# A block mask spread by GpSimd, mask rows in fewer head pairs, and token mixing moved ahead

## The chip, the cores and the metric

The kernel runs on one core of a Trainium2 chip. The metric is the device time of one execution in microseconds (us). A profile is one execution, and its span is about 2 us shorter than the device time.

The engines are PE (TensorE, matmuls), PEld (TensorE's weight loads), ACT (ScalarE), DVE (VectorE), POOL (GpSimd) and SP (SyncE).

## The reference, cut to what matters

Block-sparse attention (4 batches, 8 heads, 768 positions, head size 64) is followed by an MLP mixer over tokens and channels.

```python
scores = scale * np.matmul(q, k.transpose(0, 1, 3, 2))
blk_i, blk_j = pos[:, None] // 32, pos[None, :] // 32
mask = np.abs(blk_i - blk_j) <= 1
mask = mask | (blk_i == 0) | (blk_j == 0) | (blk_i == n_blocks - 1) | (blk_j == n_blocks - 1)
for qb in range(n_blocks):                       # three sampled key blocks per query block
    for kb in sampled_blocks[qb]:
        mask[qb*32:(qb+1)*32, kb*32:(kb+1)*32] = True
attn = softmax(np.where(mask, scores, -1e9))
x = (attn @ v)                                   # then to (batch, position, 512)
h = np.maximum(xt @ w_tok1, 0.0) @ w_tok2        # xt: x transposed, mixing of positions
u = x + h.transpose(0, 2, 1)
out = u + np.maximum(u @ w_ch1, 0.0) @ w_ch2     # mixing of channels
```

The mask is made of blocks: all positions of one query block have the same mask column.

## The kernel before: the parts that matter

The 32 heads are worked in 16 pairs. One pair has 9 attention steps, one exponential each, 144 in all. I number the steps from 1 and the pairs from 0. A batch is four pairs.

The mask is applied in two ways. In the first `NT0 = 6` pairs the scores matmul has 24 more contraction rows, which add a large negative number where a key block is not allowed. From pair 6 on, the scores have only 64 rows. Two heads' matmuls then share the array, two steps are issued together, and VectorE multiplies the exponentials by a 0/1 tile, `mask`.

```python
ev = P.op(("act",), {"act": 948.0}, [done], exp, prio=0, lat=80.0)
if p >= NT0:
    def cut(eng):                                # the mask product
        nc.vector.tensor_tensor(out=ets[s]..., in0=ets[s]..., in1=free(mask[...]), op=ALU.mult)
    ev = P.op(("dve",), {"dve": 740.0}, [ev, mask_there], cut, prio=5)
```

That tile comes from 12 matmuls of 384 columns, each with an eviction by VectorE:

```python
def mask_stream():
    for j in range(NC):                          # 6
        for hf in range(2):
            ...
                nc.tensor.matmul(out=box["m"][:, 0:384], lhsT=ind[R, j, :],
                                 rhs=qtb[0][R, 0, 384 * hf : 384 * hf + 384], ...)
            ...
                nc.vector.tensor_scalar(out=mask[:, j, 384 * hf : 384 * hf + 384],
                                        in0=box["m"][:, 0:384], scalar1=-1.0, ..., op0=ALU.is_ge)
```

The order of instructions on each engine is fixed when the kernel is built. A planner steps through estimated time. TensorE takes work from the stream with the lowest number that is ready: scores 0, PV 1, transposes 2, token mixing 3, channel mixing 4, mask 1.8. Loads go into one list, which GpSimd issues in order:

```python
for p in range(4, NP):
    loads.append(p)                              # k, q, v of pair p, when their buffers are free
    if p == 5:
        loads.append(load_ch1)                   # weights of the first channel matmul
    if p == 7:
        loads.append(load_ch2)                   # weights of the second
```

In the traces each engine then does its list in order, and if one instruction waits, what stands behind it on that engine waits too: the 1.23 us wait of one VectorE copy, shown below, holds up the two adds behind it.

The softmax here doesn't subtract the row's maximum and nothing guards it: scores larger than these inputs give would overflow.

Of the kernel before, what the change touches and what calls it, by code (L numbers as in the profile page):

```python
# [50 lines left out]
class Planner:  # L51
# [52 lines left out]
    def step(self):  # L104
# [3 lines left out]
        if self.free_at["pe"] <= self.now:  # L108
            for s in self.streams:
# [11 lines left out]
                if t <= self.now:  # L121
                    s[3] = None
                    emit()
                    if self.trace is not None:
                        self.trace.append((self.now, "pe", s[0], cost))
                    self.free_at["pe"] = self.now + cost
                    if done is not None:
                        done.t = self.now + cost + self.PE_LAT + self.SEM
                    moved = True
                    break  # L130
# [43 lines left out]
def kernel(  # L174
# [12 lines left out]
    nc = tc.nc  # L187
# [11 lines left out]
    NT0 = 6  # L199
# [226 lines left out]
    rows_there = {p: Ev(START) for p in range(NV)}  # L426
    ones_there = [Ev(START) for _ in range(NV)]

    def first_rest():
# [33 lines left out]
        rows_there[0] = e2_there  # L463
        for n in range(1, NV):
# [10 lines left out]

    mask = sb1.tile([128, NC, S], BF16, name="mask")
    mask_there = Ev()

    def mask_stream():

        for j in range(NC):
            for hf in range(2):
                box, last, rel = {}, Ev(), Ev()

                def emit(j=j, hf=hf, box=box, rel=rel):
                    P.take("pm", rel)
                    box["m"] = psM.tile([128, 512], FP32, tag="pm", name=f"pm_mask_{j}_{hf}")
                    nc.tensor.matmul(  # L488
                        out=box["m"][:, 0:384], lhsT=ind[R, j, :],
                        rhs=qtb[0][R, 0, 384 * hf : 384 * hf + 384], start=True, stop=True,  # L490
                    )

                yield 162.5, [Ev(34 * US), rows_there[0]], [("pm", 1)], emit, last

                def copy(eng, j=j, hf=hf, box=box):
                    nc.vector.tensor_scalar(
                        out=mask[:, j, 384 * hf : 384 * hf + 384], in0=box["m"][:, 0:384],
                        scalar1=-1.0, scalar2=None, op0=ALU.is_ge,
                    )

                ev = P.op(("dve",), {"dve": 556.0}, [last], copy, prio=4)
                rel.same_as = ev
        mask_there.same_as = ev
# [124 lines left out]
    def scores(s, done, rel):  # L628
# [24 lines left out]
        if p >= NT0:  # L653
            def cut(eng):
                nc.vector.tensor_tensor(  # L655
                    out=ets[s][:, :, :].rearrange("k h (i q) -> k h i q", i=2),
                    in0=ets[s][:, :, :].rearrange("k h (i q) -> k h i q", i=2),
                    in1=free(mask[:, 2 * jj, 256 * t : 256 * t + 256], 0, [[0, 2], [S, 2], [1, 256]]),
                    op=ALU.mult,
                )  # L660

            ev = P.op(("dve",), {"dve": 740.0}, [ev, mask_there], cut, prio=5)
# [40 lines left out]
    def pv_stream():  # L703
        for s in steps:
# [3 lines left out]
            def emit(s=s, done=done):  # L708
# [39 lines left out]
                ev = P.op(("dve",), {"dve": 630.0}, [done], norm, prio=1)  # L748
# [42 lines left out]
    def tok(b, g):  # L791
        deps = [x_there[2 * g + 4 * b + i, h] for i in range(2) for h in range(3)] + [tok1_there]
        box = {}
# [19 lines left out]
        a_there = relu_op(lambda: a_t[:, :, :], box["pm"][:, :, :], [last], 3)  # L813
        alias(rel, a_there)
        u_evs = []
        for s2 in range(3):
# [22 lines left out]
            ev = P.op(("dve",), {"dve": 695.0}, [last], add, prio=3)  # L839
# [6 lines left out]
        for dmc in (2 * g, 2 * g + 1):  # L846
# [25 lines left out]
            ev = P.op(("dve", "act"), {"dve": 555.0, "act": 740.0}, [last], evac, prio=3)  # L872
# [86 lines left out]
    def tok_stream():  # L959
        for b in range(B):  # L960
# [10 lines left out]
    P.stream(3, tok_stream())  # L971
# [5 lines left out]
    for p in range(4, NP):  # L977
# [3 lines left out]
        if p == 7:  # L981
            loads.append(load_ch2)

    def pull():
        while loads:
            x = loads[0]
            if callable(x):
                x(P.now)
# [42 lines left out]
```

## Time and profile before

| | before |
|---|---|
| device time, median of 3 runs | 263.84 us (263.08 to 264.56) |
| span of the profile | 261.9 us |
| busy share PE / DVE / ACT / POOL | 97% / 66% / 69% / 16% |
| mask matmuls and their evictions | 12 of 384 columns, 12 x 549 ns on VectorE |
| mask products on VectorE | 90 x 682 ns |
| granted TensorE clock, mean | 1.000 |

The chain of work that ended last shows what the end time hangs on. The timeline of ScalarE shows when each attention step ran and what it waited for. The waits say which instruction stood, and on what.

### The profile page before, as it was taken

What the parts mean: (1) busy time and instruction counts of PE and PEld (TensorE: products, weight loads), DVE (VectorE), ACT (ScalarE), POOL (GpSimd) and SP (SyncE); (2) the same over time, 40 slices, a digit from 0 to 9 for tenths busy, and PEclk for the clock granted to TensorE, in tenths of its full rate; (3) what the DMA queues carried; (4) which work ended last, traced back from release to release, by engine and by line L of the source; (5) the groups of instructions that cost most, each with busy time, mean ns of one, the idle gap of its engine ahead of it and who ended that gap; (6) DMA issues with size and microseconds to landing.
All of it is one profiled execution on the core that took longest, in us unless ns stands there. A gap on an engine that the chain in (4) does not pass through costs nothing.

```text
span 261.9 us, 6584 instructions
## 1 busy us (share of the span) xinstructions
PE 253.7 (97%) x2769; PEld 166.3 (63%) x2787; DVE 172.2 (66%) x386; ACT 179.4 (69%) x227; POOL 42.0 (16%) x66
## 2 busy tenths in 40 slices
PE   8898999999999999999999999999999999999994
PEld 3587987897766666567556765566565554565444
DVE  7887788787988889788888888888841012200222
ACT  5899999999887887677777887777407730177100
POOL 8845555462303010000000000000000000000000
PEclk9999999999999999999999999999999999999999
DMA  6999999999665726141735030015214003200122
GB/s 145 191 216 202 213 201 206 204 200 190 92 100 78 98 33 120 44 103 40 167 99 40 3 60 3 0 43 103 78 46 100 0 8 115 94 28 3 40 107 95
DMA packets 39262, 25.58 MB, mean 98 GB/s; under 512 B 20480, under 2 KB 35600, under 8 KB 39232
## 3 DMA queue, kind: packets, MB, share of 16 engines
q0 software_dynamic: 15104, 12.98, 31.7%
q1 hardware_dynamic: 23856, 11.97, 19.4%
q8 instruction: 22, 0.36, 0.6%
q10 hardware_dynamic: 272, 0.20, 0.3%
q14 instruction: 8, 0.07, 0.1%
HBM read 26.74 MB, written 6.29 MB: 126 GB/s over the span
## 4 chain that ended last, share of the span: by engine, by line
PE 85%; DMA 6%; DVE 4%; POOL 2%; issue 1%; POOLq 0%
PE pm_ch L893 24%; PE pm_ch L919 23%; PE ps L637 15%; PE po L723 13%; DMA vraw<-in_v_dram 6%; PE pm_tok L801 4%; PE pm_tok L826 4%; PE pm_mask L488 1%; DVE x L834 1%; DVE et L655 1%; PE tk L579 1%; PE tq L579 1%; PE pm_ut L855 0%; DVE x L738 0%; DVE ktb L608 0%
## 5 line engine op out<-in xcount | busy, mean ns | idle before, releaser
L647 ACT ACTIVATE et<-ps 128x1024 bf16<-128x1024 f32 x144 | 139.1, 1024 | 28.0 <-PE ps L637 26.7
L893 PE MATMUL pm_ch<-uT,w_ch 128*128 128x384 bf16 x384 | 70.1, 326 | 0.0
L919 PE MATMUL pm_ch<-w_ch,rc 128*128 128x512 bf16 (+2 forms) x294 | 67.0, 362 | 1.1 <-issue 0.3
L637 PE MATMUL ps<-qtb,ktb 64*128 64x256 bf16 (+1 forms) x576 | 60.4, 272 | 1.1 <-ACT et L647 0.7
L723 PEld LDWEIGHTS <-et 128*128 128x128 bf16 x1152 | 49.3, 97 | 17.0 <-issue 3.1
L655 DVE TENSOR_TENSOR et<-et,mask 128x1024 bf16<-128x1024 bf16 x90 | 57.8, 682 | 0.0
L723 PE MATMUL po<-vaug,et 128*128 128x65 bf16 x1152 | 56.1, 193 | 1.2 <-DVE x L738 0.8
L765 ACT ACTIVATE rc<-pm_ch 128x384 bf16<-128x384 f32 x69 | 33.8, 492 | 26.9 <-PE pm_ch L893 26.7
L931 DVE TENSOR_TENSOR o<-pm_ch,x 128x512 f32<-128x512 f32 x23 | 15.8, 687 | 52.6 <-PE pm_ch L919 52.6
L893 PEld LDWEIGHTS <-w_ch 128*128 128x128 bf16 x384 | 35.4, 98 | 22.0 <-issue 2.2
L637 PEld LDWEIGHTS <-ktb 64*128 64x128 bf16 (+1 forms) x576 | 32.6, 95 | 18.5 <-issue 13.5
L919 PEld LDWEIGHTS <-rc 128*128 128x128 bf16 x312 | 27.5, 98 | 24.8 <-issue 1.3
L738 DVE TENSOR_TENSOR x<-po,recip 128x256 bf16<-128x256 f32 x48 | 20.4, 424 | 1.7
L737 DVE RECIPROCAL recip<-po 128x4 f32<-128x4 f32 x48 | 8.7, 181 | 19.3 <-PE po L723 18.8
L834 DVE TENSOR_TENSOR x<-pm_tok,x 128x512 bf16<-128x512 f32 x24 | 15.7, 682 | 4.1 <-PE pm_tok L826 4.1
L234 POOL DMA_DIRECT2D vraw<-in_v_dram x16 | 11.6, 727 | 32.7 <-DVE vaug L525 27.8
L767 DVE TENSOR_SCALAR rc<-pm_ch 128x384 bf16<-128x384 f32 x27 | 14.8, 552 | 2.2 <-PE pm_ch L893 1.8
L826 PE MATMUL pm_tok<-a_t,w_tok 128*128 128x256 bf16 x96 | 14.1, 276 | 0.2
L801 PE MATMUL pm_tok<-x,w_tok 128*128 128x256 bf16 x96 | 13.6, 273 | 0.0
L234 POOL DMA_DIRECT2D qraw<-in_q_dram x15 | 10.8, 721 | 8.0 <-DMA w_tok<-in_moe_w_tok_dram 1.9
L234 POOL DMA_DIRECT2D kraw<-in_k_dram x15 | 10.8, 719 | 7.0 <-DVE klay L528 1.8
L826 PEld LDWEIGHTS <-w_tok 128*128 128x128 bf16 x96 | 9.9, 128 | 1.5 <-issue 1.0
(71 smaller groups left out, 116.1 us busy)
## 6 DMA issues: line engine op xcount, KB each, us to landing
out_dram<-o SPq DMA_DIRECT2D x23, 256.0 KB, 2.1
vraw<-in_v_dram POOLq DMA_DIRECT2D x16, 192.0 KB, 7.1
w_ch<-in_moe_w_ch_dram POOLq DMA_DIRECT2D x8, 384.0 KB, 9.9
kraw<-in_k_dram POOLq DMA_DIRECT2D x15, 192.0 KB, 8.3
qraw<-in_q_dram POOLq DMA_DIRECT2D x15, 192.0 KB, 7.3
w_tok<-in_moe_w_tok_dram POOLq DMA_DIRECT2D x2, 384.0 KB, 9.8
kf<-in_k_dram SPq DMA_DIRECT2D x2, 192.0 KB, 3.0
ktb<-ktb SPq DMA_DIRECT2D x3, 72.0 KB
```

The source lines that it names most:

```text
L234: nc.gpsimd.dma_start(out=raw[:, :, :, :], in_=APx(src, 2 * p * S * D, [[NC * D, 128], [S * D, 2], [1, NC * D]]),)
L637: nc.tensor.matmul(out=ps[:, hd, 256 * i : 256 * i + 256], lhsT=ktb[n][rows, h, 256 * jj + 128 * i : 256 * jj + 128 * i + 128], rhs=qtb[n] ...
L647: nc.scalar.activation(out=et[:, :, :], in_=ps[:, :, :], func=AF.Exp, scale=0.125)
L655: nc.vector.tensor_tensor(out=ets[s][:, :, :].rearrange("k h (i q) -> k h i q", i=2), in0=ets[s][:, :, :].rearrange("k h (i q) -> k h i q" ...
L723: nc.tensor.matmul(out=po[:, hd, c, :], lhsT=et[:, hd, 256 * i + 128 * c : 256 * i + 128 * c + 128], rhs=va[:, hd, 2 * jj + i, 0:65], star ...
L738: nc.vector.tensor_tensor(out=free(xs[b][:, pb // 2, 2 * t, 128 * (pb % 2) : 128 * (pb % 2) + 128], 0, [[64, 2], [256, 2], [1, 64]],), in0 ...
L765: nc.scalar.activation(out=o(), in_=i, func=AF.Relu)
L801: nc.tensor.matmul(out=box["pm"][:, t, :], lhsT=w_tok1[:, sc, 128 * t : 128 * t + 128], rhs=xs[b][:, g, sc, :], start=(t == 0 and sc == 0) ...
L826: nc.tensor.matmul(out=ubox["pm"][:, i, :], lhsT=w_tok2[:, t, :, 2 * s2 + i], rhs=a_t[:, t, :], start=(i == 0 and t == 0), stop=(i == 1 an ...
L834: nc.vector.tensor_tensor(out=st[b]["u"][:, g, 2 * s2 : 2 * s2 + 2, :], in0=ubox["pm"][:, :, :], in1=xs[b][:, g, 2 * s2 : 2 * s2 + 2, :], ...
L893: nc.tensor.matmul(out=pbox["pm"][:, 0:384], lhsT=w_ch1[:, dmc, 128 * cc : 128 * cc + 128], rhs=st[b]["uT"][:, dmc // 2, 3 * sh : 3 * sh + ...
L919: nc.tensor.matmul(out=pbox["pm"][:, 0:n], lhsT=box["rc"][:, cc, 128 * sc : 128 * sc + 128], rhs=w_ch2[:, cc, lo : lo + n], start=(cc == 0 ...
```

## The change

The intent is to take work from TensorE. One mask matmul per key chunk makes only 24 columns, one per query block. GpSimd copies each into its 32 positions, in 18 copies. The mask rows stay only for batch 0 (`NT0 = 4`), so pairs 4 and 5 get the cheaper scores and a mask product. The token mixing of batch 0 moves ahead of PV and of the transposes, and its evictions ahead of the norms (`urgent`), so that channel mixing can start earlier. One line in the planner makes a stream's next item known at once, and two of its cost estimates change (mask product 740 to 695 ns, norm 630 to 610), which can shift the order that it finds.

```diff
+                    s[3] = next(s[2], False)
-    NT0 = 6
+    NT0 = 4
...
+    maskb = sb1.tile([128, NC, 24], BF16, name="maskb")
...
+            for j in range(NC):
+                nc.tensor.matmul(
+                    out=box["m"][:, j, :], lhsT=ind[R, j, :],
+                    rhs=free(qtb[0][R, 0, 5 * 128 : 5 * 128 + 1], 0, [[16, 8], [5, 3]]),
...
+    def spread_mask(i):
+        def do(t):
+            cuts = ((0, 6, 11, 16), (0, 5, 11, 16), (0, 5, 10, 16))[i]
+            for c in (2 * i, 2 * i + 1):
+                for b in range(3):
+                    lo, n = cuts[b], cuts[b + 1] - cuts[b]
+                    nc.gpsimd.tensor_copy(
+                        out=free(mask[:, 0, 128 * c + lo : 128 * c + lo + 1], 0,
+                                 [[S, NC], [16, 8], [1, n]]),
+                        in_=free(maskb[:, 0, b : b + 1], 0, [[24, NC], [3, 8], [0, n]]),
...
+        urgent = 0.5 if b == 0 else 3        # ReLU, adds and evictions of the token mixing
...
-    P.stream(3, tok_stream())
+    P.stream(0.5, tok_stream((0,)))
+    P.stream(3, tok_stream((1, 2, 3)))
...
         if p == 7:
             loads.append(load_ch2)
+        if 5 <= p <= 7:
+            loads.append(spread_mask(p - 5))
```

The last two lines put the copies into the list from which GpSimd issues the loads.

More of the change, by code (lines that the diff above doesn't have):

```diff
@@ L426 @@
     rows_there = {p: Ev(START) for p in range(NV)}
+    built = set()
     ones_there = [Ev(START) for _ in range(NV)]
@@ L463, in first_rest @@
         rows_there[0] = e2_there
+        built.add(("row", 0))
         for n in range(1, NV):
@@ L476 @@
     mask = sb1.tile([128, NC, S], BF16, name="mask")
-    mask_there = Ev()
+    maskb = sb1.tile([128, NC, 24], BF16, name="maskb")
+    maskb_there, mask_there = Ev(), Ev()
     def mask_stream():
-        for j in range(NC):
-            for hf in range(2):
-                box, last, rel = {}, Ev(), Ev()
-                def emit(j=j, hf=hf, box=box, rel=rel):
-                    P.take("pm", rel)
-                    box["m"] = psM.tile([128, 512], FP32, tag="pm", name=f"pm_mask_{j}_{hf}")
-                    nc.tensor.matmul(
-                        out=box["m"][:, 0:384], lhsT=ind[R, j, :],
-                        rhs=qtb[0][R, 0, 384 * hf : 384 * hf + 384], start=True, stop=True,
-                    )
-                yield 162.5, [Ev(34 * US), rows_there[0]], [("pm", 1)], emit, last
-                def copy(eng, j=j, hf=hf, box=box):
-                    nc.vector.tensor_scalar(
-                        out=mask[:, j, 384 * hf : 384 * hf + 384], in0=box["m"][:, 0:384],
-                        scalar1=-1.0, scalar2=None, op0=ALU.is_ge,
-                    )
-                ev = P.op(("dve",), {"dve": 556.0}, [last], copy, prio=4)
-                rel.same_as = ev
-        mask_there.same_as = ev
@@ new lines, in mask_stream, with emit @@
+        box, last, rel = {}, Ev(), Ev()
+        def emit():
+            P.take("pm", rel)
+            box["m"] = psM.tile([128, NC, 24], FP32, tag="pm", name="pm_mask")
+            for j in range(NC):
+                nc.tensor.matmul(
+                    out=box["m"][:, j, :], lhsT=ind[R, j, :],
+                    rhs=free(qtb[0][R, 0, 5 * 128 : 5 * 128 + 1], 0, [[16, 8], [5, 3]]),
+                    start=(j == 0), stop=(j == NC - 1),
+                )
+        yield lambda: ("row", 0) in built
@@ new lines, in mask_stream, with copy @@
+        yield 330.0, [rows_there[0]], [("pm", 1)], emit, last
+        def copy(eng):
+            nc.vector.tensor_scalar(
+                out=maskb[:, :, :], in0=box["m"][:, :, :],
+                scalar1=-1.0, scalar2=None, op0=ALU.is_ge,
+            )
+        maskb_there.same_as = P.op(("dve",), {"dve": 306.0}, [last], copy, prio=4)
+        rel.same_as = maskb_there
+    def spread_mask(i):
[8 more added lines that the diff above has]
+                        in_=free(maskb[:, 0, b : b + 1], 0, [[24, NC], [3, 8], [0, n]]),
+                    )
+            if i == 2:
+                mask_there.t = t + 4 * US
+        return do
@@ L660, in cut @@
                 )
-            ev = P.op(("dve",), {"dve": 740.0}, [ev, mask_there], cut, prio=5)
+            ev = P.op(("dve",), {"dve": 695.0}, [ev, mask_there], cut, prio=5)
         alias(et_there[s], ev)
@@ L746, in norm @@
                     )
-                ev = P.op(("dve",), {"dve": 630.0}, [done], norm, prio=1)
+                ev = P.op(("dve",), {"dve": 610.0}, [done], norm, prio=1)
                 alias(rel, ev)
@@ L812, in tok @@
         a_t = sbw.tile([128, 2, 256], BF16, tag="a_t", name=f"a_t{b}_{g}")
-        a_there = relu_op(lambda: a_t[:, :, :], box["pm"][:, :, :], [last], 3)
+        a_there = relu_op(lambda: a_t[:, :, :], box["pm"][:, :, :], [last], urgent)
         alias(rel, a_there)
@@ L837, in add @@
                 )
-            ev = P.op(("dve",), {"dve": 695.0}, [last], add, prio=3)
+            ev = P.op(("dve",), {"dve": 695.0}, [last], add, prio=urgent)
             alias(rel, ev)
@@ L870, in evac @@
                     nc.vector.tensor_copy(out=o, in_=i)
-            ev = P.op(("dve", "act"), {"dve": 555.0, "act": 740.0}, [last], evac, prio=3)
+            ev = P.op(("dve", "act"), {"dve": 555.0, "act": 740.0}, [last], evac, prio=urgent)
             alias(rel, ev)
@@ L957, in tr_stream, with tok_stream @@
             yield from transposes(p)
-    def tok_stream():
-        for b in range(B):
+    def tok_stream(bs):
+        for b in bs:
             for g in range(2):
@@ L987, in pull @@
             if callable(x):
-                x(P.now)
+                if maskb_there.t is None:
+                    return
+                x(max(P.now, maskb_there.t))
             else:
```

## The prediction

> **What bounds the kernel now.** I read the page first: busy shares, then the chain that ended last.
>
> ```profile
> PE 253.7 (97%) x2769; PEld 166.3 (63%) x2787; DVE 172.2 (66%) x386; ACT 179.4 (69%) x227; POOL 42.0 (16%) x66
> ...
> PE 85%; DMA 6%; DVE 4%; POOL 2%; issue 1%; POOLq 0%
> PE pm_ch L893 24%; PE pm_ch L919 23%; PE ps L637 15%; PE po L723 13%; DMA vraw<-in_v_dram 6%; PE pm_tok L801 4%; PE pm_tok L826 4%; PE pm_mask L488 1%; DVE x L834 1%; DVE et L655 1%; PE tk L579 1%; PE tq L579 1%; PE pm_ut L855 0%; DVE x L738 0%; DVE ktb L608 0%
> ```
>
> TensorE looks saturated, but its busy time is modelled and matmuls overlap, so 97% does not say how much room is left. To see that I need the interval at which TensorE really issues each kind of work. The chain in order of time gives it, because a piece there runs from one end to the next:
>
> ```profile
> 43.00 0.44 PE ps L637 x4
> 43.44 0.24 PE po L723 x8
> 43.68 0.27 PE pm_mask L488
> ...
> 44.77 0.43 PE pm_mask L488 x2
> ...
> 80.35 0.54 PE ps L637 x8
> 80.89 0.92 PE pm_ch L893 x5
> ...
> 195.96 15.85 PE pm_ch L893 x96
> 212.07 10.74 PE pm_ch L919 x49
> ```
>
> One attention step (128 keys twice, 256 queries, two heads) costs 0.44 us for scores with the mask rows (4 matmuls of 88 rows). From pair 6 on, two steps together cost 0.54 us for 8 matmuls of 64 rows; the 5 channel matmuls after them should take 5 x 15.85/96 = 0.83 us and take 0.92, so I book 0.65 for two steps with the changeover. PV costs 0.24 per step, the first channel matmul 0.165, the second 0.219, a mask matmul alone 0.27 and two 0.43. Token mixing comes to 0.109 per matmul (12 in 1.31), a transpose to 0.056.
>
> Now the stages, by one attention step = one exponential. I counted in the instruction order of the built kernel how much TensorE work lies ahead of the scores of step 36, 66 and 144, and read from the ScalarE timeline when those steps ran (42.2, 73.7 and 185.2 us):
>
> ```profile
> 25.96 16.70 ACT L647 ACTIVATE et<-ps 128x1024 bf16<-128x1024 f32 x17 [0.62 <-PE ps L637]
> 42.85 6.10 ACT L647 ACTIVATE et<-ps 128x1024 bf16<-128x1024 f32 x6 [0.19 <-PE ps L637]
> ...
> 121.14 1.94 ACT L647 ACTIVATE et<-ps 128x1024 bf16<-128x1024 f32 x2 [0.20 <-PE ps L637]
> 123.82 1.94 ACT L647 ACTIVATE et<-ps 128x1024 bf16<-128x1024 f32 x2 [0.74 <-PE ps L637]
> ```
>
> Up to step 54 the exponentials run back to back (17 in 16.70 us): ScalarE sets the pace and TensorE has holes. From about 75 us ScalarE waits 0.7 us before each pair of exponentials: TensorE sets the pace. The tally: start to step 36, 35.7 us for 31.1 us of TensorE work (4.6 idle); step 36 to 66, 31.5 us for 29.7 (1.8 idle); step 66 to 144, 111.5 us for 110.0 (1.5 idle); the rest 76.7 us for 72.9, with the last eviction and store at the end (3.8). So the end time is TensorE work, about 243.7 us, plus 6.5 us of start-up, 3.8 of tail and some 7.9 us of holes, nearly all before step 66.
>
> **What the Trainium skill says.** "Perfetto Trace Analysis", Identifying the Most-Contended Engine, says matmul busy share does not measure distance to the limit; the trace agrees (a score matmul shows 272 ns in the groups, but is issued every 109 ns). "TensorEngine Tiling (Array Packing)", Theoretical Speedup, gives up to 2x for a contraction of at most 64; the chain shows 0.88 us against 0.54 for two steps, 1.6x, or 1.35x with the changeover. "GPSIMD Engine Reference", Engine selection, calls one-input elementwise work on GpSimd roughly line-rate; before has no GpSimd copy, but its 24x768 select took 856 ns and its 128x128 one 292 ns, 0.88 ns per element and 0.18 fixed. "SBUF — State Buffer", Who interferes with whom, says GpSimd shares a port pair with VectorE's fast SBUF copies and with two-input operations from SBUF, and the second to start is blocked for the whole instruction. No run here shows that yet; the q, k, v copies (350 ns) and the mask product (682 ns) are such operations.
>
> **The change part by part.**
>
> Removed from TensorE: 12 mask matmuls of 384 columns, 1.1% of the chain or 2.9 us (6 alone at 0.27, 3 twos at 0.43). Added: 6 of 24 columns, an estimated 0.3 us at the pace of a small matmul. Pairs 4 and 5 (18 steps) lose the mask rows: 18 x 0.44 = 7.9 becomes 9 x 0.65 = 5.9. TensorE loses 2.6 + 2.0 = 4.6 us of 243.7.
>
> ```profile
> L655 DVE TENSOR_TENSOR et<-et,mask 128x1024 bf16<-128x1024 bf16 x90 | 57.8, 682 | 0.0
> ...
> L496 DVE TENSOR_SCALAR mask<-pm_mask 128x384 bf16<-128x384 f32 x12 | 6.3, 549 | 0.5 <-PE pm_mask L488 0.5
> ```
>
> VectorE gains 18 mask products: 18 x 0.682 = 12.3 us. It loses 12 mask evictions (6.3, less about 0.3 for the small one) and, for pairs 4 and 5, eight half evictions that become four whole ones of 0.55 (2.2; some of them ScalarE's). Net about +4 us of 172, but moved: the mask evictions lay at steps 29 to 41, the products lie at steps 37 to 54.
>
> GpSimd gains 18 copies of 240 or 288 elements per partition: 0.18 + 0.88 x 288/1000 = 0.43 us each, an estimate, about 8 us, in three batches of 2.5 between its load issues. The loads for pairs 6, 7 and 8 are issued that much later, up to 7 us. But in 20 to 60 us the transfers run at 204 GB/s and land a median 8 to 10 us after issue, so the queue holds a backlog, and the copies mostly fill time in which GpSimd waited anyway. Pair 7 is now transposed at step 38 instead of 44, so that is where a late load would show first.
>
> Moved: in the instruction order the first token mixing of batch 0 is whole by step 27 instead of 42, the second by step 42 instead of 60, and at step 66 already 84 of the first channel matmuls are done, where before had 4. That is about 13 us of TensorE work brought ahead of step 66.
>
> What the move is worth is only the holes that it closes. Holes before step 36 stay (4.6): nothing of the channel mixing can start there. Steps 36 to 48 now come in twos with little channel work yet: TensorE has 12.7 us of work there, ScalarE 12 exponentials (11.3), three evictions (2.4), a ReLU (0.6) and some 0.2 us before each two (1.2), 15.5 us; VectorE is as full (norm 12 to norm 16: about 17 us of intervals for 15 us of TensorE work). So about 3 us of holes arise. Steps 48 to 66 have 26 us of TensorE work for 18 exponentials: dense, 0.3 us. Holes before step 66 then 4.6 + 3.0 + 0.3 = 7.9, against 6.4: 1.5 us more.
>
> Sum: -4.6 + 1.5 + 0.3 for port blocking = -2.8 us as the cautious figure. If the tenth that VectorE operations overlap one another takes VectorE out of the way, and holes stay as they were or shrink a little, it is -4.6 to -5. I take -3.9: **259.9 us**, ratio 0.985.
>
> **Rivals.** (1) *VectorE takes the place of TensorE.* Steps 36 to 60 would hold 25 mask products, 15 ReLU evictions and the second token mixing within some 26 us; for it, VectorE durations between norm 12 and norm 18 sum to 29.8 us. Against it: before's norms 18 to 24 have the same 29.8 us and took 25.5, as neighbours overlap (three mixing adds in 1.87 us, 682 each). If it bites, 262 to 263. (2) *GpSimd hurts*: copies of 1 us rather than 0.43, with short runs of 5 or 6 elements, would delay pair 7's load past step 38 and block VectorE; TensorE, in fixed order, would stand. For it: the pattern is unlike any measured here. Cost 2 to 4 us, 262 to 264. (3) *The holes close*: early channel work also lets the dense stage start before 60 us, and the token work ahead of step 30 costs ScalarE nothing. Holes fall to about 5 and the time to 256.5 or 257. For it: from 54 us on TensorE has work for every pair; against: ScalarE's floor in 36 to 48. (4) *Nothing moves*: the mask matmuls lay in ScalarE's stage, so removing them buys nothing by itself; only work pulled forward turns them into time. Then 262.
>
> **Range and chances.** The work removed from TensorE is sure; the holes are not, by 3 us either way. Eight in ten: 257.2 to 262.8. Faster by over 2% means below 258.6, for which rival 3 must hold mostly: 0.24. Slower by over 2% means over 269.1 and needs a stall that no row shows: 0.03. Else within 2%.
>
> **What would show it.** The 12 mask matmuls and evictions gone, mask products 108 with a mean still near 682 ns (more than 720 would be port blocking); GpSimd copies near 0.43 us; the exponentials of steps 65 and 66 later than before's 74.3 us by some 10 (more work lies ahead of them) and the scores of step 144 later than 185.2 by some 7, while the rest after them shrinks by 10 (24 more first and 29 more second channel matmuls done by then: 24 x 0.165 + 29 x 0.219). First channel matmuls dense from about 58 us instead of 75. I am wrong if step 36 itself moves by over 1 us, if VectorE shows no idle time before the norms in 45 to 75 us, or if a q, k copy waits for its DMA in 35 to 50 us.

## The result, and the profile after

| | before | after |
|---|---|---|
| device time, median of 4 runs | 263.63 us (263.08 to 264.56) | 260.87 us (260.51 to 261.37) |
| span of the profile | 261.9 us | 259.3 us |

The ratio is 0.9893, with a 95% interval of 0.986 to 0.9927: 1.1% faster, within the 2% that counts as the same. Here and below a ratio is the mean time of one kernel's fast runs over that of the other's of the same rounds, so it is not quite the ratio of the medians that I quote.

The page of after, its busy shares and the chain that ended last:

```profile
PE 248.7 (96%) x2760; PEld 160.1 (62%) x2781; DVE 181.3 (70%) x398; ACT 175.8 (68%) x218; POOL 49.6 (19%) x84
...
PE 76%; DMA 15%; POOL 4%; DVE 2%; issue 2%
PE pm_ch L916 25%; PE pm_ch L942 24%; PE po L744 11%; PE ps L658 11%; DMA w_ch<-in_moe_w_ch_dram 4%; DMA qraw<-in_q_dram 4%; DMA kraw<-in_k_dram 4%; PE pm_tok L849 3%; PE pm_tok L824 3%; DMA vraw<-in_v_dram 3%; POOL w_ch L261 1%; DVE x L857 1%; POOL mask L517 1%; POOL vraw L235 1%; POOL kraw L235 1%
```

The mask matmuls are gone from the chain. The new thing is DMA 15% and POOL 4%, where before had 6% and 2%: the chain now runs back through loads of q, k and channel weights. That makes loads a suspect. Busy TensorE fell by one point while the span fell by 2.6 us, so the share alone tells nothing.

The mask product, from the same page's groups:

```profile
L676 DVE TENSOR_TENSOR et<-et,mask 128x1024 bf16<-128x1024 bf16 x108 | 69.9, 683 | 0.9 <-ACT et L668 0.9
```

There are 18 more products at the same mean of 683 ns: the copies do not slow the product, taken over the whole kernel. But the last copy ends at 42.2 us and the first product begins at 46.45, so here none ran beside the other.

The timeline of ScalarE after (start us, duration, instruction; in brackets the idle time just before it and its releaser):

```profile
46.80 2.01 ACT L668 ACTIVATE et<-ps 128x1024 bf16<-128x1024 f32 x2
...
49.52 1.94 ACT L668 ACTIVATE et<-ps 128x1024 bf16<-128x1024 f32 x2 [0.22 <-PE ps L658]
53.48 1.94 ACT L668 ACTIVATE et<-ps 128x1024 bf16<-128x1024 f32 x2 [2.02 <-PE ps L658]
...
84.31 1.94 ACT L668 ACTIVATE et<-ps 128x1024 bf16<-128x1024 f32 x2 [0.72 <-PE ps L658]
```

The waits before a pair of exponentials are 0.2 to 0.4 us in this stage, except for one of 2.02 us ahead of 53.48. The pair at 84.31 is steps 65 and 66, which before ran at 74.29. So at this point after is 10 us behind, and it makes that up later, as predicted.

What stands at 51 to 53 us is seen on VectorE and TensorE, in the timelines of after:

```profile
49.73 0.42 DVE L759 TENSOR_TENSOR x<-po,recip 128x256 bf16<-128x256 f32 x1
51.38 0.42 DVE L549 COPY klay<-kraw 128x768 bf16<-128x768 bf16 x1 [1.23 <-DMA kraw<-in_k_dram]
51.73 1.27 DVE L857 TENSOR_TENSOR x<-pm_tok,x 128x512 bf16<-128x512 f32 x2
```

```profile
52.46 0.60 PE L849 MATMUL pm_tok<-a_t,w_tok 128*128 128x256 bf16 x4 [1.57 <-DVE x L857]
52.99 0.61 PE L658 MATMUL ps<-qtb,ktb 64*128 64x256 bf16 x8
```

Read it from the top. VectorE has nothing to do for 1.23 us, because its next instruction copies the k of pair 8, which has not landed. The two token mixing adds stand behind that copy. The next token matmuls wait 1.57 us for the adds. The scores stand behind those matmuls on TensorE, and ScalarE waits 2.02 us for the scores. The busy shares do not show this; the releasers followed in turn do.

When the load was issued is seen on GpSimd, in the timeline of after and then of before:

```profile
30.75 2.38 POOL L517 COPY mask<-maskb 128x240 bf16<-128x240 bf16 x6
...
39.12 0.77 POOL L261 DMA_DIRECT2D w_ch<-in_moe_w_ch_dram  x1 [0.18 <-issue]
39.90 2.29 POOL L517 COPY mask<-maskb 128x240 bf16<-128x240 bf16 x6
42.13 0.74 POOL L235 DMA_DIRECT2D kraw<-in_k_dram  x1
```

```profile
39.81 0.74 POOL L234 DMA_DIRECT2D kraw<-in_k_dram  x1 [0.44 <-DVE x L738]
```

Pair 8's k is issued 2.3 us later (42.13 against 39.81), behind a batch of six copies. But it does not land 2.3 us later. The DMA view (`--dma`) of a window that holds this one issue gives its time to landing, before and then after:

```profile
kraw<-in_k_dram POOLq DMA_DIRECT2D x1, 192.0 KB, 11.0
```

```profile
kraw<-in_k_dram POOLq DMA_DIRECT2D x1, 192.0 KB, 9.2
```

So it landed at 50.8 us before and at 51.4 after, 0.5 us later. In both it landed about 1 us behind the last of the four loads of the second channel weights: it stood in the queue behind them, and a later issue only meant a shorter wait there. Nor do the copies explain the 0.5 us. The q load issued at 20.5 us, ahead of the first copy at 25.9, already landed 0.7 us later than before's, and in e1 and e2, which have the same copies, pair 8's k landed at 50.4 and 50.9. What changed is when it is needed, about 6 us sooner: before copied it at 56.07 us, 5.2 us after it had landed, and after has that copy next in line from 50.15.

The end of the chain of after, in order of time:

```profile
223.84 15.60 PE pm_ch L916 x96
...
255.08 0.29 DVE o L961
```

The same two pieces began at 227.34 and 258.58 before: the dense end is unchanged and begins 3.5 us sooner.

A profile's span carries noise that has nothing to do with this. From the start of the last eviction to the end of the span took 2.9 to 4.7 us over the profiles, in no order that follows the edits (3.3 before, 4.2 after). In some profiles the granted clock also dips to between 0.82 and 0.92 for a while near 6.5 to 20 us. So beside the device times I use a **stretch** of the trace that leaves both of these out: from the start of step 36's exponential to the start of the last VectorE eviction. It is 258.58 - 42.85 = 215.73 us before and 255.08 - 42.72 = 212.36 after.

### The profile page after: what moved, and what is told of

Read it like the earlier page. It is cut to its first block, busy times and chain, and to the rows that moved or that the text cites. A ratio compares the mean times of both kernels' runs of the same rounds, so it can differ in the third digit from the quotient of the medians.

```text
span 259.3 us, 6595 instructions
## 1 busy us (share of the span) xinstructions
PE 248.7 (96%) x2760; PEld 160.1 (62%) x2781; DVE 181.3 (70%) x398; ACT 175.8 (68%) x218; POOL 49.6 (19%) x84
## 4 chain that ended last, share of the span: by engine, by line
PE 76%; DMA 15%; POOL 4%; DVE 2%; issue 2%
PE pm_ch L916 25%; PE pm_ch L942 24%; PE po L744 11%; PE ps L658 11%; DMA w_ch<-in_moe_w_ch_dram 4%; DMA qraw<-in_q_dram 4%; DMA kraw<-in_k_dram 4%; PE pm_tok L849 3%; PE pm_tok L824 3%; DMA vraw<-in_v_dram 3%; POOL w_ch L261 1%; DVE x L857 1%; POOL mask L517 1%; POOL vraw L235 1%; POOL kraw L235 1%
## 5 line engine op out<-in xcount | busy, mean ns | idle before, releaser
L916 PE MATMUL pm_ch<-uT,w_ch 128*128 128x384 bf16 x384 | 73.0, 326 | 0.1
L676 DVE TENSOR_TENSOR et<-et,mask 128x1024 bf16<-128x1024 bf16 x108 | 69.9, 683 | 0.9 <-ACT et L668 0.9
L744 PEld LDWEIGHTS <-et 128*128 128x128 bf16 x1152 | 47.9, 97 | 18.3 <-DVE x L759 3.1
L658 PE MATMUL ps<-qtb,ktb 64*128 64x256 bf16 (+1 forms) x576 | 54.7, 272 | 1.3 <-ACT et L668 0.9
L744 PE MATMUL po<-vaug,et 128*128 128x65 bf16 x1152 | 54.6, 193 | 1.4 <-DVE x L759 1.1
L916 PEld LDWEIGHTS <-w_ch 128*128 128x128 bf16 x384 | 34.4, 98 | 21.2 <-issue 3.2
L786 ACT ACTIVATE rc<-pm_ch 128x384 bf16<-128x384 f32 x58 | 28.6, 492 | 25.6 <-PE pm_ch L916 25.5
L658 PEld LDWEIGHTS <-ktb 64*128 64x128 bf16 (+1 forms) x576 | 29.3, 95 | 20.3 <-issue 14.8
L788 DVE TENSOR_SCALAR rc<-pm_ch 128x384 bf16<-128x384 f32 x38 | 21.1, 555 | 6.1 <-PE pm_ch L916 5.4
L824 PE MATMUL pm_tok<-x,w_tok 128*128 128x256 bf16 x96 | 12.9, 273 | 0.0
```

What stands on the lines that cost most here:

```text
L658: nc.tensor.matmul(out=ps[:, hd, 256 * i : 256 * i + 256], lhsT=ktb[n][rows, h, 256 * jj + 128 * i : 256 * jj + 128 * i + 128], rhs=qtb[n] ...
L676: nc.vector.tensor_tensor(out=ets[s][:, :, :].rearrange("k h (i q) -> k h i q", i=2), in0=ets[s][:, :, :].rearrange("k h (i q) -> k h i q" ...
L744: nc.tensor.matmul(out=po[:, hd, c, :], lhsT=et[:, hd, 256 * i + 128 * c : 256 * i + 128 * c + 128], rhs=va[:, hd, 2 * jj + i, 0:65], star ...
L786: nc.scalar.activation(out=o(), in_=i, func=AF.Relu)
L788: nc.vector.tensor_scalar(out=o(), in0=i, scalar1=0.0, scalar2=None, op0=ALU.max)
L824: nc.tensor.matmul(out=box["pm"][:, t, :], lhsT=w_tok1[:, sc, 128 * t : 128 * t + 128], rhs=xs[b][:, g, sc, :], start=(t == 0 and sc == 0) ...
```

## The experiments

All are timed in 5 rounds against the kernel before. Diffs are against the kernel after unless said otherwise. They ran on three chips, one for e1 to e4 (median of before 263.75), one for e5, e6, e7 and e9 (263.59), and one for e10 to e12 (263.95) and e13 (264.26, with one more run of before). The change itself was timed only with its result, so against it the runs below are compared over the ratio to before, and by its one profile.

Three theories stood for the part of the predicted gain that did not come. *Late load*: pair 8's k comes too late. *VectorE full*: the 18 added mask products keep VectorE from its other work (rival 1 of the prediction). *Two at a time* (theory S): issuing pairs 4 and 5 two steps at a time makes ScalarE stand.

### e1: the spread alone

```diff
-    NT0 = 4
+    NT0 = 6
-        urgent = 0.5 if b == 0 else 3
+        urgent = 3
-    P.stream(0.5, tok_stream((0,)))
-    P.stream(3, tok_stream((1, 2, 3)))
+    P.stream(3, tok_stream((0, 1, 2, 3)))
```

> The mask product tile spread by GpSimd as in the change, but mask rows for pairs 0 to 5 and the token mixing of batch 0 in its old place. TensorE loses only the 12 mask matmuls (some 2.5 us of issue time), and those lay where ScalarE sets the pace. Theory (time = TensorE work + holes): only work pulled ahead counts; the instruction order has 14 first channel matmuls ahead of step 66 instead of 4, 1.6 us, so ratio near 0.994 (262.1 us). Rival A (mask matmuls on the path, all of them count): 0.990. Rival B (they lay in holes, nothing counts): 1.000. Rival C (GpSimd copies hurt through the shared port or late loads): 1.005 or more.

Measured: 262.63 us, ratio 0.997 (0.9924 to 1.0016). The stretch is 256.26 - 41.73 = 214.53, 1.2 us shorter than before's. About 2.6 us of TensorE work were taken out, and less than half shows in the trace; the device time alone does not tell it from nothing. This run also has the planner's new line and cost estimates, so it is not quite the spread alone.

### e2: spread and fewer mask rows, token mixing in its old order

```diff
-        urgent = 0.5 if b == 0 else 3
+        urgent = 3
-    P.stream(0.5, tok_stream((0,)))
-    P.stream(3, tok_stream((1, 2, 3)))
+    P.stream(3, tok_stream((0, 1, 2, 3)))
```

> The whole change but for the order of batch 0's token mixing, which stays behind PV. TensorE loses the full 4.6 us; 76 first channel matmuls lie ahead of step 66 (84 in the change). Theory: nearly the whole gain, ratio 0.990 to 0.992. Rival (the earlier token mixing is what opens the work, without it no gain): 0.998 to 1.000.

Measured: 261.41 us, ratio 0.9907 (0.9873 to 0.9942), stretch 255.97 - 42.14 = 213.83. So the token order is worth 1.5 us in the trace of the change (213.83 against 212.36), though the device times do not tell the two apart. Against e13 below, where no load is late, it is 2.8 us (213.83 against 210.99). VectorE waits for no k in e1 and e2, but 0.5 us for a q (at 51.43 and 52.40).

### e3: the token order alone, on the kernel before

```diff
+                    s[3] = next(s[2], False)
+        urgent = 0.5 if b == 0 else 3
-    P.stream(3, tok_stream())
+    P.stream(0.5, tok_stream((0,)))
+    P.stream(3, tok_stream((1, 2, 3)))
```

> The kernel before with only the token mixing of batch 0 ahead of PV and norms (and the planner's line that fetches a stream's next item at once). TensorE work unchanged; 60 first channel matmuls lie ahead of step 66 instead of 4. Theory: only holes can close, at most the 1.8 us between steps 36 and 66, ratio 0.994 to 1.000. Rival (the order is the main part): 0.990 or less.

Measured: 265.19 us, ratio 1.0046 (1.0011 to 1.0081), stretch 260.12 - 43.69 = 216.43, 0.7 us longer than before's. Alone, this part makes the kernel slower. The timelines of ScalarE and VectorE of e3:

```profile
41.61 12.45 ACT L648 ACTIVATE et<-ps 128x1024 bf16<-128x1024 f32 x12
...
58.98 0.79 ACT L607 COPY ktb<-tk 64x768 bf16<-64x768 bf16 x1 [0.85 <-PE tk L580]
```

```profile
58.54 0.56 DVE L497 TENSOR_SCALAR mask<-pm_mask 128x384 bf16<-128x384 f32 x1 [0.18 <-PE pm_mask L489]
```

The exponentials stop at 54.06 and begin again only at 61.69. In between the last of the 12 mask evictions is at 58.54, where before had finished them by 49.7: the token work was put in front of them, and the transposes of the next pair came after. That they stood one for the other is inferred from this order; e4 is the test, as it has no such evictions (but it has the planner's new cost estimates, which e3 lacks).

### e4: the change with mask rows in six pairs

```diff
-    NT0 = 4
+    NT0 = 6
```

> The whole change but with mask rows for pairs 0 to 5 as before: TensorE loses 2.5 us instead of 4.6, VectorE gets no added mask products before step 54, 40 first channel matmuls ahead of step 66. Theory: about 2 us above the change if the packed scores of pairs 4 and 5 pay in full, but the change lost some 1.3 us of new holes in steps 36 to 48 that this one does not have, so 0.5 to 1 us above: ratio 0.992. Rival (VectorE bounds the change, so its 18 added products cost more than the packing gives): 0.986 to 0.989, faster than the change.

Measured: 259.72 us, ratio 0.9851 (0.9816 to 0.9885), stretch 254.02 - 42.22 = 211.80. The same place in its ScalarE timeline:

```profile
38.36 22.41 ACT L668 ACTIVATE et<-ps 128x1024 bf16<-128x1024 f32 x23 [0.45 <-PE ps L658]
```

There are 23 exponentials without a stop, across the time at which e3 stood. e4 is e1 plus the token order, which takes 2.7 us off here (214.53 to 211.80) and added 0.7 in e3. The two parts are worth more together than apart. Also, the part that was booked with 2.0 us of TensorE time, fewer mask rows, is worth nothing in the change: without it the stretch is 0.6 us shorter (the intervals of the device times overlap). e4 waits for no k load in this stage.

### e5: the second channel weights one place later in the list

```diff
-        if p == 7:
+        if p == 8:
             loads.append(load_ch2)
```

> The change with the load of the second channel weights issued after pair 8's loads instead of before them, so pair 8's k lands some 5 us earlier. In the change VectorE waited 1.23 us for it at 50 to 51 us, TensorE then 1.6 us and ScalarE 2.0 us. Theory L (a late load makes the new holes of steps 36 to 66): 1.2 to 1.6 us faster than the change, ratio 0.983 to 0.985. Theory V (VectorE is full with the 18 added products) and theory S (ScalarE waits at each two steps): no faster than the change by more than 0.3 us, ratio 0.988 to 0.990.

Measured: 259.78 us, ratio 0.984 (0.9818 to 0.9862), stretch 254.41 - 43.46 = 210.95, which is 1.4 us shorter than the change's. This is what the late load predicts. But the planner sees the load's place in the list, so the order of other work shifts as well; e13 mends that.

### e6: no mask products in pairs 4 and 5 (wrong)

```diff
             def cut(eng):
+                if p < 6:
+                    return
```

The result is wrong by design (relative error 0.285): those pairs are not masked.

> The change without the 18 mask products of pairs 4 and 5, same order on every engine otherwise; the result is wrong on purpose (those pairs attend everywhere). It takes 12.3 us of VectorE work out of steps 37 to 54. Theory V: the 3.6 us of holes of steps 36 to 66 shrink by 2 or more, ratio 0.980 to 0.982. Theory L: VectorE still stands at pair 8's load, at most 0.5 us, ratio 0.987 to 0.989. Theory S: the same as L.

Measured: 259.96 us, ratio 0.9871 (0.9848 to 0.9895), stretch 255.02 - 42.72 = 212.30 against 212.36. Taking 18 x 0.683 = 12.3 us off VectorE buys 0.06 us. One reservation: the wait for pair 8's k is 1.8 us here instead of 1.2, as VectorE reaches it sooner, so up to 0.6 us may hide there. VectorE full is rejected as the cause of the missing gain.

### e7: each GpSimd copy twice

```diff
-                    nc.gpsimd.tensor_copy(
+                    for _ in range(2):
+                        nc.gpsimd.tensor_copy(
```

> The change with each of the 18 GpSimd copies done twice (7.5 us more on GpSimd, same values). Theory L: the loads of pairs 6 to 8 are issued 2.5, 5 and 7.5 us later, pair 8's wait grows from 1.2 to some 5 us or pair 7's begins, and the time grows by 3 us or more, ratio 0.999 or more. Theory V or S alone, with the loads hidden behind the queue's backlog: ratio 0.989 to 0.992. If the copies block VectorE through the shared port, q, k, v copies near them get longer than 350 ns.

Measured: 267.88 us, ratio 1.0153 (1.0134 to 1.0172), stretch 261.40 - 42.97 = 218.43. VectorE's timeline:

```profile
47.65 3.31 DVE L677 TENSOR_TENSOR et<-et,mask 128x1024 bf16<-128x1024 bf16 x4
...
56.55 0.36 DVE L550 COPY klay<-kraw 128x768 bf16<-128x768 bf16 x1 [5.05 <-DMA kraw<-in_k_dram]
```

The same copy now waits 5.05 us, and the next exponentials 6.2. The copies now take 18.5 us of GpSimd in place of 8.4, pair 8's k is issued at 52.82 us and lands at 56.5, 5.2 us later than in the change, and the stretch is 6.1 us longer. From 38 to 42 us the transfers of the change and of e7 were these (columns as explained under e11; the last is GB/s):

```profile
38.00:42.00 4.00, 3.95 (x74) 3.57 (x71) 3.30 (x11) 3.45 (x5) 3.65 (x8) 1.00 1.29 204
```

```profile
38.00:42.00 4.00, 4.00 (x77) 3.50 (x74) 3.86 (x10) 3.38 (x4) 3.79 (x8) 1.00 0.20 27
```

With the copies done once, the loads issued earlier kept the transfers going at 204 GB/s; with twice the copies they ran dry. So in this kernel the copies fit into the slack of the queue once, and not twice. The first line of the timeline shows a second effect: four mask products took 3.31 us while copies ran (a group mean of 842 ns from 20 to 60 us, against 683). VectorE also waits for q here (1.0 us at 45.72, 0.7 at 58.80), and the granted clock falls to 0.55 from 54 to 58 us, while TensorE stands; so the k load is not all of the 6.1 us.

### e9: pairs 4 and 5 packed, but one step at a time

```diff
-            if p < NT0:
+            if p < 6:
...
-                    436.0, qk_deps(*s), [("ps", 1), ("et", 1)],
+                    436.0 if p < NT0 else 380.0, qk_deps(*s), [("ps", 1), ("et", 1)],
```

> The change, but pairs 4 and 5 issue their packed scores one step at a time, as the masked pairs do, instead of two steps together. Theory S (ScalarE stands at each two because both score buffers must come free): the exponentials of steps 37 to 54 run closer together, near 1.0 us a step, and the time falls by 1 us or more, ratio 0.982 to 0.985. Theories L and V: as the change, 0.988 to 0.991, since one step at a time pays the changeover twice as often.

Measured: 259.13 us (258.56 to 259.46), ratio 0.9821 (0.9801 to 0.9841), stretch 253.55 - 42.60 = 210.95. This is the lowest ratio measured, and its interval lies below the change's; those of e4 and e5 overlap it. But the cause is not the one I had built it for. Its new order puts pair 8's k copy at about 56 us, so its load is in time too, and its stretch equals that of e5. Whether the steps go in twos is not shown to matter by itself.

### e10: e9 with the later channel weights

```diff
+            (e9)
-        if p == 7:
+        if p == 8:
             loads.append(load_ch2)
```

> The change with packed scores of pairs 4 and 5 one step at a time and with pair 8's loads ahead of the second channel weights: both repairs at once. The one-at-a-time run alone had no wait for a load left, so it holds the gain of both. If the late load was half of what it gained (theories L and S both true, one repair already covering the load): as that run, ratio 0.981 to 0.983. If the two repairs are independent and add: 0.977 to 0.979.

Measured: 260.31 us, ratio 0.9854 (0.9822 to 0.9885), stretch 254.45 - 43.50 = 210.95, the same as e9's. Two repairs of the same wait do not add. In device time it came out 1.2 us longer than e9, on another chip. The profiles place the difference ahead of step 36, at 43.50 against 42.60, with a granted clock of 0.92 and 0.83 in two stretches near 6.5 to 20 us, where e9 had 1.00. The intervals of the ratios overlap, so I do not call e10 slower.

### e11: e4 with the later channel weights

```diff
-    NT0 = 4
+    NT0 = 6
-        if p == 7:
+        if p == 8:
             loads.append(load_ch2)
```

> Mask rows for pairs 0 to 5 (the run that was faster than the change) with pair 8's loads ahead of the second channel weights. In that run no VectorE copy waited for a load between 40 and 80 us, because pair 8 is needed some 6 us later there. Theory L says the repair is then worth nothing: ratio 0.984 to 0.986, as without it. If issuing those weights later helps for another reason: 0.981 or less, and then the run with the late weights does not speak for the late load.

Measured: 260.95 us, ratio 0.9892 (0.9858 to 0.9926), stretch 255.12 - 43.32 = 211.80, as in e4. Where there was no late load there is nothing to repair: the control comes out as it should. The profile is 1.1 us behind e4's from step 36 on, and constantly so. The stretches before that, of e4 and then of e11 (from:to in us, length, busy time of each engine, then the granted clock, DMA share and GB/s):

```profile
6.50:13.00 6.50, 5.68 (x71) 3.91 (x70) 5.72 (x15) 5.75 (x7) 5.45 (x8) 1.00 1.26 196
```

```profile
6.50:13.00 6.50, 5.66 (x52) 3.89 (x51) 5.66 (x16) 5.26 (x6) 5.12 (x8) 0.86 1.20 182
```

With the clock at 0.86, 52 matmuls were done where e4 did 71; less was transferred too (182 against 196 GB/s), so which came first is not shown. Executions of before differ likewise on the first call's chip: two with a mean clock of 0.986 and 0.987 took 265.48 and 265.55 us, one at 1.0 took 263.11. But on another chip one at 1.0 took 266.58, so the clock is not all of the scatter. No edit here was shown to cause it.

### e12: mask rows in two pairs

```diff
-    NT0 = 4
+    NT0 = 2
...                                  # pairs 2 to 5 one step at a time as in e9
-        if p == 5:
+        if p == 6:
             loads.append(load_ch1)
-        if p == 7:
+        if p == 8:
             loads.append(load_ch2)
-        if 5 <= p <= 7:
-            loads.append(spread_mask(p - 5))
+        if p == 4:
+            loads += [spread_mask(0), spread_mask(1), spread_mask(2)]
```

> The combined repair carried further: mask rows for pairs 0 and 1 only, packed scores one at a time for pairs 2 to 5, all 18 GpSimd copies right after pair 4's loads, first channel weights after pair 6's loads. TensorE work falls by 2 us more, VectorE gets 18 more products in the stage that ScalarE paces. If TensorE work is all: ratio 0.975 to 0.977. If the early stage is ScalarE's anyway (TensorE's 2 us lie in holes and nothing can be pulled ahead before batch 0 is done) or VectorE or a late load stands: 0.981 or more.

Measured: 269.26 us, ratio 1.0202 (1.0172 to 1.0232). It is the slowest of all, though it has the mask rows in the fewest pairs and so the least TensorE work. From its waits (us in total, times, longest):

```profile
DVE klay L549 <- DMA kraw<-in_k_dram: 4.1, 3, 2.0
```

The mask is now needed when the loads of the first pairs are also wanted (my reading, not tested). VectorE waits for k three times, and step 36 is reached at 50.73 us, 8 us later than in the change. This kernel changes several things at once; it shows that the idea carried further fails, not which of its edits costs most.

### e13: only the issue of the second channel weights moved

The planner is told the same landing times as in the change, so the order of every other engine is identical to the change's (the recorded sequences of TensorE, VectorE and ScalarE agree one for one). Only GpSimd issues the four loads after those of pair 8.

```diff
     def load_ch2(t):
         for i in range(4):
+            ch2_there[i].t = landing(t, 128 * DC * 2).t
+
+    def issue_ch2(t):
+        for i in range(4):
             nc.gpsimd.dma_start(
...
-            ch2_there[i].t = landing(t, 128 * DC * 2).t
...
+        if p == 8:
+            loads.append(issue_ch2)
```

> The change with the instruction order of TensorE, VectorE, ScalarE and SyncE kept to the letter; only GpSimd issues the four loads of the second channel weights after pair 8's three loads instead of before them. The earlier run with late weights also moved some matmuls, so it did not test theory L alone. Theory L: VectorE's wait of 1.23 us for pair 8's k and ScalarE's of 2.0 us vanish, and from step 36's exponential to the last eviction the trace takes 210.5 to 211.3 us instead of the change's 212.4; ratio 0.983 to 0.986. If L is wrong (the reordered matmuls made the gain): 212 us or more, ratio 0.988 to 0.991.

Measured: 260.49 us, ratio 0.9858 (0.9826 to 0.989), stretch 253.73 - 42.74 = 210.99. The timelines of VectorE, ScalarE and GpSimd, to be read beside those of after:

```profile
50.09 0.35 DVE L552 COPY klay<-kraw 128x768 bf16<-128x768 bf16 x1
50.36 1.28 DVE L860 TENSOR_TENSOR x<-pm_tok,x 128x512 bf16<-128x512 f32 x2
```

```profile
52.12 1.94 ACT L671 ACTIVATE et<-ps 128x1024 bf16<-128x1024 f32 x2 [0.64 <-PE ps L661]
```

```profile
34.54 2.32 POOL L520 COPY mask<-maskb 128x240 bf16<-128x240 bf16 x6
36.78 0.72 POOL L235 DMA_DIRECT2D kraw<-in_k_dram  x1
```

Pair 8's k is issued at 36.78 instead of 42.13 and lands at 43.8 instead of 51.4, as the four loads of weights (384 KB each, landing 1.9 us apart) now come behind it. VectorE no longer waits for it, ScalarE's wait of 2.02 falls to 0.64, and the stretch is 212.36 - 210.99 = 1.37 us shorter. This isolates the late load: the wait in the change costs about 1.4 us of its stretch. The device times alone would not show it: 0.9858 against 0.9893, and the intervals overlap.

### All runs together

| kernel | ratio to before | stretch, us | wait of VectorE for a k load, 45 to 60 us |
|---|---|---|---|
| before | 1 | 215.73 | none |
| the change | 0.9893 | 212.36 | 1.2 |
| e1 spread alone | 0.997 | 214.53 | none |
| e2 without token order | 0.9907 | 213.83 | none |
| e3 token order alone | 1.0046 | 216.43 | none |
| e4 six pairs with rows | 0.9851 | 211.80 | none |
| e5 weights later | 0.984 | 210.95 | none |
| e6 no products (wrong) | 0.9871 | 212.30 | 1.8 |
| e7 copies twice | 1.0153 | 218.43 | 5.05 |
| e9 one at a time | 0.9821 | 210.95 | none |
| e10 e9, weights later | 0.9854 | 210.95 | none |
| e11 e4, weights later | 0.9892 | 211.80 | none |
| e13 issue swapped | 0.9858 | 210.99 | none |

e12 is left out, as its step 36 is 8 us late. In e13, the change and e7, whose edits touch only GpSimd's list or the copies in it, the stretch grows with the wait: 0, 1.2 and 5.05 us give 210.99, 212.36 and 218.43 (in e7 by more than the wait, for the reasons given there). How far one profile can be trusted is seen from pairs of runs. e9 and e10 have the same order on TensorE, VectorE and ScalarE, and so have e4 and e11; the change and e6 differ in the left-out products alone. Their stretches differ by 0.00, 0.00 and 0.06 us, so 1.37 us is clear of that.

## Why the prediction was right or wrong

The verdict was within 2%, given 0.73, and it was right. The time was put at 259.9 and measured at 260.87, inside the range. The gain was put at 3.9 us and came to 2.8, which equals the cautious figure of the working, but by luck: one term of that sum stood for another, as shown under the holes.

**What is removed and added.** Right. The 12 mask matmuls and their evictions are gone and there are 108 mask products at 683 ns. The predicted 0.43 us per copy is 0.491 for 240 elements and 0.496 for 288, as the groups from 20 to 60 us show:

```profile
L517 POOL COPY mask<-maskb 128x240 bf16<-128x240 bf16 x12 | 5.4, 491 | 0.0
L517 POOL COPY mask<-maskb 128x288 bf16<-128x288 bf16 x6 | 3.0, 496 | 0.0
```

Six of them took 2.3 to 2.8 us, 0.38 to 0.47 each, so the batches were as long as predicted (2.5). The total of 8.4 us agrees with 8. One term was missed: VectorE's busy time grew by 9.1 us (172.2 to 181.3) and not by about 4, as the planner now gave it 38 of the first channel evictions instead of 27 (21.1 us against 14.8). And the loads of pairs 6, 7 and 8 were issued 2.3, 3.8 and 2.3 us later, not up to 7, as GpSimd waited less between them.

**Port blocking.** What fits it is seen on the q, k and v copies. The groups of VectorE from 24 to 46 us, before and then after, for v:

```profile
L525 DVE COPY vaug<-vraw 128x768 bf16<-128x768 bf16 x3 | 1.1, 351 | 0.0
```

```profile
L546 DVE COPY vaug<-vraw 128x768 bf16<-128x768 bf16 x3 | 1.6, 522 | 0.0
```

With k (352 to 398 ns, 4 copies) and q (354 to 443, 4 copies), VectorE lost 3 x 0.171 + 4 x 0.046 + 4 x 0.089 = 1.05 us. It sits almost wholly in five single copies. Three ran beside GpSimd's copies: q at 27.70 us (724 ns), v at 28.35 (541) and k at 41.86 (549), some 0.76 us together. The other two, v at 38.51 (593) and at 42.60 (433), had only the issue of a load on GpSimd beside them, and before has one such too (v at 54.63, 591), so these are not the copies' doing. All five begin ahead of the stretch, and step 36 came no later than before (42.72 against 42.85). So the 0.3 us that I booked is neither shown nor excluded.

**The work moved.** Right. Steps 65 and 66 came at 84.31 instead of 74.29 (10.0 later; predicted some 10), and the scores of step 144 at 191.8 instead of 184.7 (7.1; predicted some 7). From there to the last eviction it was 255.08 - 191.8 = 63.3 us instead of 258.58 - 184.7 = 73.9: 10.6 less, predicted 10. Step 36 stayed where it was (42.72 against 42.85). Two readings behind this were loose without harm: the scores of step 144 ran at 184.7 before and not at 185.2, and of the two lines shown for the late stage one has a wait of 0.74 us and the other of 0.20, so ScalarE did not wait 0.7 us before each pair.

**The holes.** The size came out right by luck, as the cause was partly another. With the prediction's own weights for TensorE's work, start to step 36 took 35.3 us for 30.9 of work, and step 36 to 66 took 83.88 - 41.75 = 42.1 for 38.6 (from scores to scores on TensorE). The holes sum to 4.4 + 3.5 = 7.9 us, predicted 7.9. It gave about 3 us of them to steps 36 to 48, saying that "TensorE has 12.7 us of work there, ScalarE" 15.5, and that "VectorE is as full". In e13, with the same order and the load in time, step 36 to 66 took 82.52 - 41.78 = 40.7 us for the same work: 2.1 us of holes, where before has 1.9 by the same count. So the new order made almost no new holes; of the 1.5 us that the prediction added for them, nearly all is the late load. The exponentials say the same: from step 36 to 48 the change took 59.10 - 42.72 = 16.4 us and e13 57.74 - 42.74 = 15.0 (predicted 15.5), and steps 48 to 66 took 26.1 us in both, predicted 26 and dense.

**The step that failed** is this one: "Pair 7 is now transposed at step 38 instead of 44, so that is where a late load would show first." It looked for the late load at the wrong pair. Pair 7's k, issued ahead of the second channel weights, landed at 40.8 us and was copied at 43.67, with 2.9 us in hand. Pair 8's stands behind these weights in the queue. Before had 5.2 us in hand for it; the new order wants it 5.9 us sooner, and it landed 0.5 later, so it came 5.9 - 5.2 + 0.5 = 1.2 us too late. No term of the sum holds that. The sentence before it held: "the queue holds a backlog, and the copies mostly fill time in which GpSimd waited anyway". The 2.3 us by which the issue was later did not reach the landing. The prediction had also named the sign ("if a q, k copy waits for its DMA in 35 to 50 us"); the wait ended at 51.38 us, just outside the window it gave.

**The choice between -2.8 and -4.6 to -5.** I took the middle, crediting VectorE's overlap. The repaired kernel tells what that was worth: its stretch is 215.73 - 210.99 = 4.7 us shorter than before's, and the change's is 3.4. So the upper figure was there to be had, and the term that was missing from it is 1.4 us for the load.

**Fewer mask rows.** Booked as 2.0 us of TensorE work. With the load in time, the kernel with rows in four pairs has a stretch of 210.99, and e4 with six has 211.80: they pay 0.8 us. In the change the late load took this and more (212.36). The rest would be TensorE work that lay in ScalarE's stage, where the exponentials set the pace and removed work leaves a hole, as rival 4 put it; no run tests that.

**The rivals.** Rival 1, VectorE as the new bound, fell with e6; its sign did not show either, as VectorE was idle before two norms between 45 and 75 us (0.41 and 0.51 us). Rival 2 was right that a late load would make TensorE stand in its fixed order, but not that the copies of 0.4 to 0.5 us would make it late; e7, with every copy done twice and so about 1 us each, took 7.0 us more than the change (267.88 against 260.87), where the rival said 2 to 4, and even that is not the wait alone. Rival 3, holes that fall to about 5, did not come even in e13, which has 4.4 + 2.1 = 6.5. Rival 4 is wrong for the whole and comes nearest for e1, where 2.6 us of work removed gave 1.2 in the trace and nothing certain in the time.

What stays open: in device time the difference between the change and e13 is not clear of noise, and only the traces, one profile of each, show it. Open too is why e9's device time is below e10's although their stretches agree: the profiles show a difference of the granted clock, but no run controls it.

## What to carry to other kernels

When a change moves work ahead, look up every load: when it lands, and when its consumer stands first in line in the new order. One load checked, or a median delay of all, does not answer that. When it lands need not follow from when it was issued: behind a full queue a load issued 2.3 us later landed 0.5 us later, and putting it ahead of four loads of weights brought it in 7.6 us sooner. And parts of a change are not worth a sum: here the token order cost 0.7 us alone and gained 2.7 with the mask's evictions gone, so test each part with and without the others.

## What the Trainium skill lacked or had wrong

- "GPSIMD Engine Reference", Engine selection, calls one-input elementwise work roughly line-rate. For short copies with a repeated source the length hardly showed: 240 and 288 elements per partition took 491 and 496 ns. The fixed cost of such a copy is what a planner would want, and that section does not give it.
- "SBUF — State Buffer", Who interferes with whom, has the second to start blocked for the whole instruction, and the trace agrees: three q, k and v copies beside GpSimd's copies took 724, 549 and 541 ns, where 350 is usual, and the group of mask products in e7 that holds those beside the doubled copies has a mean of 842 ns instead of 683. Of load issues by GpSimd it says only that VectorE can hold them up. Here two VectorE copies with nothing but such an issue beside them took 593 and 433 ns (591 once in before); most others beside an issue took 350, and no run tests the cause.
- No page that I drew on puts a figure on loads that stand behind others in one queue: here loads of 192 KB landed about 1.0 us apart and those of 384 KB 1.9, and the same k load took 11.0, 9.2 and 7.0 us from issue to landing (before, the change, e13).
